# The first query products ahead of the mixing weights, and another engine and bank for the last query chunk

## The chip, the cores and the metric

The kernel runs on one core of a Trainium2 chip. The metric is the device time of one execution in microseconds (us), median of several runs. Engines are named as in the profile: PE is the matrix engine (PEld its weight loads), DVE the vector engine, ACT the scalar engine, POOL the general-purpose engine that issues most loads here, SP the engine that issues the stores.

## The reference

Two blocks follow each other. The first is attention with sorted blocks: batch 4, 8 heads, 768 positions in 8 blocks of 96, head size 64. An 8 x 8 matrix per head is normalised five times by rows and columns, and then mixes the blocks of keys and values:

```
P = sort_net
for _ in range(5):
    P = exp(P - max(P)); P = P / sum over columns; P = P / sum over rows
k_sorted = einsum('bhij,bhjcd->bhicd', P, k_blocks)      # the same for v
scores = q_blocks @ k_sorted^T / sqrt(64)
attn = softmax(scores) @ v_sorted                         # per block of 96
```

The second is a feed-forward block on the 3072 rows of 512 numbers that the attention gives:

```
g = x @ w_gate                       # 512 -> 1536
out = (g * sigmoid(g) * (x @ w_val)) @ w_out              # 1536 -> 512
```

Inputs and output are float32; the kernel casts to bf16 while loading.

## The kernel before, in words

The output is made in eight parts of 384 rows, n = 0 to 7 (a batch and a half each). For each part, `ffn(n)` runs twelve steps m of 128 hidden columns: `gate` (L385, four products into one PSUM bank), `value` (L403), and for the part before it `outp` (L420). Attention units of later parts are merged into this stream by a list of due places (`merge`). All of this is an order written out by hand: PE and POOL run exactly in program order over the whole kernel, DVE and ACT in the prologue.

The prologue makes what part 0 needs from batch 0, in this order on PE:

- `dots(124)` and groups of `fill(idle_ps, n)` (L446): products of zeros whose results nobody reads. The groups stand between single products that read `rowreds[it]` (L455), so that they follow the rounds of normalisation on DVE and ACT.
- `weights(0)`, `weights(1)` (L463): 16 products that spread the normalised matrix `p_bf` into one bank, `w_ps`. `p_bf` is written by DVE in two halves (L214).
- `mix_rows` (L468, DVE): masks `w_ps` into `rmix[0]`, the right-hand side of all value and key products of batch 0. For batches 1 to 3 the same is done later from the same bank, which therefore stays in use until then.
- `q0_chunk(0, 0, 16)` (L254): 32 products with `sel`, a matrix of ones and zeros, that bring query rows into the layout of the scores. They need the load of `q0[0]` (L142) but no mixing weights.
- `v_chunk` six times (L275), `k0_chunk` four times (L264), `q0_chunk(0, 16, 8)` (L254, 16 products), `fill(idle_ps, 4)`, and then the scores `qk` (L307).

Each chunk has a PSUM tile and ends with `drain(eng, ...)`, which copies it to SBUF: `"v"` is DVE (L222), `"s"` is ACT (L224). The last argument names the PSUM tile: `"a"` and `"b"` are pairs of banks with one buffer each, `"gen"` single banks with three buffers in turn. A chunk waits until the drain of the chunk that had its buffer is done. The last chunks of the prologue stand so:

```
k0_chunk(0, 16, "v", "a")
k0_chunk(16, 16, "s", "b")
k0_chunk(32, 8, "v", "gen")
k0_chunk(40, 8, "s", "gen")
q0_chunk(0, 16, 8, "v", "a")
fill(idle_ps, 4)
qk(0, 0, "a")
```

After the scores come exponentials on ACT (L320, L318), attention products `av` (L334), DVE's division (L338, L340), transposes (L351), and the first gate and value products (L519).

POOL issues the loads in program order: the first value rows, `q0[0]` (L142), the first key rows (L149), three copies of value rows (L124), and then the weights of `gate` and `value` in twelve loads of 256 columns (L111), with other loads between. The last two of them hold the columns of steps m = 10 and 11. After the first few, each issue waits until an older load has landed.

Of the kernel before, what the change touches and what calls it, by code (L numbers as in the profile page):

```python
# [17 lines left out]
def kernel(  # L18
# [201 lines left out]
    def drain(eng, dst, src):  # L220
        if eng == "v":
            nc.vector.tensor_copy(dst, src)  # L222
        else:
            nc.scalar.copy(dst, src)  # L224
# [3 lines left out]
    def kqt_tile(b):  # L228
        if b not in kqts:
            kqts[b] = kqp.tile([128, 2 * H2 * NB * C + 32], BF16, name=f"kqt{b}", tag="kqt")  # L230
        return kqts[b]
# [3 lines left out]
    def chunk_tile(name, n, tag):  # L235
        return pair_tile(name, tag) if n == 2 else bank_tile(name, tag)
# [12 lines left out]
    def q0_chunk(t, at, n, eng, tag):  # L249
        dst = kqt_tile(0)[:, GI * C:2 * GI * C].rearrange("p (g t r c) -> p t g r c", g=H2, t=2, c=QC)[:, t]  # L250
        tp = chunk_tile("tq0", n // 8, tag).rearrange("p (l g r) -> p l g r", l=n, g=H2)
        for lc in range(n):
            for two in range(2):
                nc.tensor.matmul(tp[two * D:(two + 1) * D, lc], lhsT=q0[t][:, at + lc, :],  # L254
                                 rhs=sel[:, two], start=True, stop=True)
        drain(eng, dst[:, :, :, at:at + n], tp.rearrange("p l g r -> p g r l"))

    def k0_chunk(at, n, eng, tag):
        dst = kqt_tile(0)[:, 0:GI * C].rearrange("p (n a c) -> p a n c", a=2, c=HC)
        rm = rmix[0].rearrange("p a (g two) i -> p two a g i", two=2)  # L260
        tp = chunk_tile("tk0", n // 8, tag).rearrange("p (l a n) -> p l a n", l=n, a=2)
        for lc in range(n):
            for two in range(2):
                nc.tensor.matmul(tp[two * D:(two + 1) * D, lc].rearrange("p a (g i) -> p a g i", g=H2),  # L264
                                 lhsT=k0[:, at + lc, :], rhs=rm[:, two], start=True, stop=True)
        drain(eng, dst[:, :, :, at:at + n], tp.rearrange("p l a n -> p a n l"))

    def v_chunk(b, at, n, eng, tag):
        rows = slice(0, 128) if b % 2 else lowr
        dst = vt_tile(b // 2)[:, b % 2]  # L270
        mix = rmix[b][rows, 0].rearrange("p a b -> p (a b)")
        tp = chunk_tile("tv", n // 8, tag).rearrange("p (l n) -> p l n", n=H * NB)
        for ld in range(n):
            col = (at + ld) * C
            nc.tensor.matmul(tp[:, ld, :], lhsT=vch[rows, col:col + 128], rhs=mix,  # L275
                             start=True, stop=True)
        drain(eng, dst[:, :, at:at + n], tp[0:C].transpose([0, 2, 1]))
# [166 lines left out]
    def fill(tile, n):  # L444
        for _ in range(n):
            nc.tensor.matmul(tile, lhsT=warm_sb[:, 0:128], rhs=warm_sb, start=True, stop=True)  # L446

    def dots(n):
        for _ in range(n):
            nc.tensor.matmul(idle_ps[0:32, 0:32], lhsT=warm_sb[:, 0:32], rhs=warm_sb[:, 0:32],  # L450
                             start=True, stop=True)

    dots(124)
    for it, n in ((1, 3), (2, 4), (3, 4), (4, 4)):
        nc.tensor.matmul(idle_ps[0:NB, 0:NB], lhsT=rowreds[it][:, :, 0], rhs=rowreds[it][:, :, 0],  # L455
                         start=True, stop=True)
        fill(idle_ps, n)
# [3 lines left out]
    def weights(half):  # L461
        for i in range(NB):
            nc.tensor.matmul(w_ps[halves[half], i].rearrange("p b h -> p (b h)"),  # L463
                             lhsT=p_bf[:, i].rearrange("p a b -> p (a b)"),
                             rhs=ident[0:BH, 0:BH], start=True, stop=True)

    def mix_rows(dst, rows, b):
        nc.vector.tensor_tensor(dst, mask[rows].unsqueeze(2).to_broadcast([R, H, NB]),  # L468
                                w_ps[rows, :, b].transpose([0, 2, 1]), op=ALU.mult)

    weights(0)
    weights(1)
    mix_rows(rmix[0][lowr, 0], lowr, 0)
    mix_rows(rmix[0][highr, 1], highr, 0)
    q0_chunk(0, 0, 16, "s", "b")
    v_chunk(0, 0, 8, "v", "gen")
    v_chunk(0, 8, 8, "s", "gen")
    v_chunk(0, 16, 16, "v", "a")
# [4 lines left out]
    k0_chunk(16, 16, "s", "b")  # L483
    k0_chunk(32, 8, "v", "gen")
    k0_chunk(40, 8, "s", "gen")
    q0_chunk(0, 16, 8, "v", "a")
    fill(idle_ps, 4)
    qk(0, 0, "a")
    qk(0, 1, "b")
# [165 lines left out]
```

## Time and profile before

| | |
|---|---|
| median of 3 runs | 248.58 us (248.43 to 248.70) |
| the profiled execution | 249.62 us |
| its span (first to last instruction) | 247.7 us |
| PE busy | 239.4 us, 97% of the span |
| DVE busy | 157.1 us, 63% |
| ACT busy | 109.5 us, 44% |
| POOL busy | 51.9 us, 21% |
| DMA | 24.38 MB, mean 98 GB/s |

Times in the trace count from the start of the span. A row of the timeline gives start and length, engine, line, operation and tiles, and in brackets how long the engine had been idle before it and which event ended that. Rows that follow each other with the same line and form are put together, with their number behind an x. Products on PE are pipelined: a row's length holds one full latency, and the next row starts before it ends. The profiled execution is one run with the profiler on; its own time stands beside its span because other runs need not agree with it in every part.

### The profile page before, as it was taken

Reading aid. Unit: us, or ns where it says so; the run is one execution under the profiler, and the core shown is the slowest. Engines: PE = TensorE matmul, PEld = TensorE weight load, DVE = VectorE, ACT = ScalarE, POOL = GpSimd, SP = SyncE. Lnnn points to the kernel's source line nnn. Section 1 sums busy time; section 2 is a strip of 40 time slices with the busy share of each in tenths; the row PEclk is TensorE's granted clock in tenths of the full one; section 3 lists DMA queues with packets and bytes.
Section 4 is the critical chain, followed back from the end, with each engine's and each line's share of the span. In section 5 each row is a group of like instructions: output and inputs, shape, how many; then the busy total and the mean of one; then the engine's idle time right before and its main releaser. Section 6 shows DMA issues by size and latency. Waiting matters only on the chain.

```text
span 247.7 us, 6185 instructions
## 1 busy us (share of the span) xinstructions
PE 239.4 (97%) x2633; PEld 140.7 (57%) x2633; DVE 157.1 (63%) x332; ACT 109.5 (44%) x186; POOL 51.9 (21%) x45
## 2 busy tenths in 40 slices
PE   8799998999999999999999999999999999999995
PEld 6375665666555556655555655565555555555543
DVE  6686789787556775857657646755764585446700
ACT  3877652453544444444642552354245334232311
POOL 5993459960049300000000000000000000000000
PEclk9999999999999999999999999999999999999999
DMA  5999999999999287010122121112111121100122
GB/s 98 214 120 181 218 191 219 194 227 215 215 164 179 41 201 173 4 42 3 45 56 52 55 62 34 44 42 78 32 42 45 39 57 54 42 21 25 42 81 88
DMA packets 39578, 24.38 MB, mean 98 GB/s; under 512 B 27712, under 2 KB 35648, under 8 KB 39104
## 3 DMA queue, kind: packets, MB, share of 16 engines
q0 software_dynamic: 21376, 14.16, 39.3%
q1 hardware_dynamic: 18176, 9.84, 13.9%
q8 instruction: 20, 0.33, 0.5%
q14 instruction: 6, 0.05, 0.1%
HBM read 28.32 MB, written 7.86 MB: 146 GB/s over the span
## 4 chain that ended last, share of the span: by engine, by line
PE 83%; DVE 9%; ACT 2%; issue 2%; DMA 2%; DVEq 0%; POOLq 0%
PE v_ps L403 23%; PE o_ps L420 23%; PE g_ps L385 22%; PE tkq L244 3%; PE av_ps L334 2%; PE qk L307 2%; DVE st L340 2%; DMA v<-in_v_dram 2%; DVE gs_sb L395 2%; DVE h L408 2%; DVE vt L222 1%; PE o_ps L436 1%; PE idle_ps L446 1%; PE tv L275 1%; ACT th_sb L393 1%
## 5 line engine op out<-in xcount | busy, mean ns | idle before, releaser
L395 DVE SCALAR_TENSOR_TENSOR gs_sb<-th_sb,g_ps 128x384 bf16<-128x384 bf16 x96 | 52.8, 550 | 51.5 <-ACT th_sb L393 48.7
L403 PE MATMUL v_ps<-xt,wv_sb 128*128 128x384 bf16 x380 | 77.3, 326 | 1.1 <-DVE st L340 0.7
L385 PE MATMUL g_ps<-xt,wg_sb 128*128 128x384 bf16 x376 | 76.7, 326 | 0.1
L393 ACT ACTIVATE th_sb<-g_ps 128x384 bf16<-128x384 f32 x96 | 47.1, 490 | 57.0 <-PE g_ps L385 54.5
L420 PE MATMUL o_ps<-wo_sb,h 128*128 128x512 bf16 x276 | 64.0, 379 | 0.0
L408 DVE SCALAR_TENSOR_TENSOR h<-v_ps,gs_sb 128x384 bf16<-128x384 f32 x96 | 53.3, 555 | 6.9
L403 PEld LDWEIGHTS <-wv_sb 128*128 128x128 bf16 x380 | 35.1, 97 | 24.9 <-issue 1.9
L385 PEld LDWEIGHTS <-wg_sb 128*128 128x128 bf16 x376 | 34.7, 97 | 23.5 <-issue 0.4
L420 PEld LDWEIGHTS <-h 128*128 128x128 bf16 x276 | 26.3, 98 | 28.9
L425 ACT COPY o_sb<-o_ps 128x512 f32<-128x512 f32 x23 | 13.5, 585 | 50.9 <-PE o_ps L420 50.9
L124 POOL COPY vch<-v 64x1536 bf16<-64x1536 bf16 (+2 forms) x11 | 28.6, 2635 | 21.1 <-DMA v<-in_v_dram 21.0
L320 ACT ACTIVATE e_all<-qk 96x768 bf16<-96x768 f32 x30 | 22.6, 802 | 7.6 <-PE qk L307 7.6
L340 DVE TENSOR_TENSOR st<-av_ps,r_sb 96x512 bf16<-96x512 f32 x32 | 21.7, 679 | 0.2
L334 PEld LDWEIGHTS <-e_all 96*128 96x128 bf16 x256 | 12.0, 97 | 4.9 <-ACT e_all L320 0.9
L334 PE MATMUL av_ps<-vt,e_all 96*128 96x65 bf16 x256 | 13.2, 193 | 0.0
L222 DVE CAST vt<-tv 96x1024 bf16<-96x1024 f32 (+1 forms) x9 | 9.8, 1096 | 2.6 <-PE tv L285 1.6
L338 DVE RECIPROCAL r_sb<-av_ps 96x8 f32<-96x8 f32 x32 | 6.4, 199 | 8.0 <-PE av_ps L334 7.9
L224 ACT CAST vt<-tv 96x1024 bf16<-96x1024 f32 (+1 forms) x9 | 8.1, 913 | 3.0 <-PE tv L285 1.8
L446 PE MATMUL idle_ps<-warm_sb 128*128 128x512 bf16 x25 | 7.7, 416 | 0.0
L222 DVE COPY oh_sb<-o_ps 128x256 f32<-128x256 f32 x1 | 0.4, 423 | 9.3 <-PE o_ps L436 9.3
L122 ACT COPY vch<-v 64x768 bf16<-64x768 bf16 (+1 forms) x4 | 5.4, 1375 | 0.7 <-DMA v<-in_v_dram 0.7
L370 POOL DMA_DIRECT2D q_scr<-in_q_dram x2 | 5.7, 3228 | 0.0
(80 smaller groups left out, 135.3 us busy)
## 6 DMA issues: line engine op xcount, KB each, us to landing
out_dram<-o_sb SPq DMA_DIRECT2D x23, 256.0 KB, 2.0
v<-in_v_dram POOLq DMA_DIRECT2D x3, 768.0 KB, 19.9
wg_sb<-in_moe_w_gate_dram POOLq DMA_DIRECT2D x6, 256.0 KB, 11.1
wv_sb<-in_moe_w_val_dram POOLq DMA_DIRECT2D x6, 256.0 KB, 11.9
wo_sb<-in_moe_w_out_dram POOLq DMA_DIRECT2D x1, 1536.0 KB, 23.8
kp<-in_k_dram POOLq DMA_DIRECT2D x2, 768.0 KB, 15.1
q_scr<-in_q_dram POOLq DMA_DIRECT2D x2, 768.0 KB, 29.9
v<-in_v_dram POOLq DMA_DIRECT2D x2, 384.0 KB, 6.4
```

The lines of the kernel that those rows point to most:

```text
L124: eng.tensor_copy(dst, src.transpose([0, 2, 1]))
L222: nc.vector.tensor_copy(dst, src)
L320: nc.scalar.activation(e_all[:, n:n + 2, 0:4 * C], wide[0:C, :, 0:4 * C], AF.Exp, scale=scale)
L334: nc.tensor.matmul(o[:, two, i4, 0:D + 1], lhsT=e[:, i4 * C:i4 * C + 128], rhs=vt[:, 2 * g + two, half * 4 + i4, 0:D + 1], start=True, sto ...
L340: nc.vector.tensor_tensor(st.rearrange("p i two d -> p two i d"), o[0:C, :, :, 0:D], r_sb.to_broadcast([C, 2, 4, D]), op=ALU.mult)
L385: nc.tensor.matmul(g_ps, lhsT=wg_sb[:, kc, ts(m, 128)], rhs=xt[:, kc, :], start=(kc == 0), stop=(kc == NKC - 1))
L393: nc.scalar.activation(th_sb, g_ps, AF.Tanh, scale=0.5)
L395: nc.vector.scalar_tensor_tensor(gs_sb, th_sb, 1.0, g_ps, op0=ALU.add, op1=ALU.mult)
L403: nc.tensor.matmul(v_ps, lhsT=wv_sb[:, kc, ts(m, 128)], rhs=xt[:, kc, :], start=(kc == 0), stop=(kc == NKC - 1))
L408: nc.vector.scalar_tensor_tensor(h_tiles[n][:, m, :], v_ps, 0.5, gs_tiles.pop(m), op0=ALU.mult, op1=ALU.mult)
L420: nc.tensor.matmul(o_ps, lhsT=h_w[:, m, ts(t3, 128)], rhs=wo_sb[:, m, :], start=(m == 0), stop=(m == NFC - 1))
L425: nc.scalar.copy(o_sb, o_ps)
```

## The change

The group of unread products after the last round of normalisation shrinks from four to one. `q0_chunk(0, 0, 16, "s", "b")` moves from behind the mixing rows to ahead of `weights(0)`, with its engine and its banks as before. The last query chunk of the prologue, `q0_chunk(0, 16, 8)`, is drained by ACT in place of DVE and takes a bank of `"gen"` in place of the pair `"a"`.

```diff
     dots(124)
-    for it, n in ((1, 3), (2, 4), (3, 4), (4, 4)):
+    for it, n in ((1, 3), (2, 4), (3, 4), (4, 1)):
         nc.tensor.matmul(idle_ps[0:NB, 0:NB], lhsT=rowreds[it][:, :, 0], rhs=rowreds[it][:, :, 0],
                          start=True, stop=True)
         fill(idle_ps, n)
...
+    q0_chunk(0, 0, 16, "s", "b")
     weights(0)
     weights(1)
     mix_rows(rmix[0][lowr, 0], lowr, 0)
     mix_rows(rmix[0][highr, 1], highr, 0)
-    q0_chunk(0, 0, 16, "s", "b")
     v_chunk(0, 0, 8, "v", "gen")
...
     k0_chunk(40, 8, "s", "gen")
-    q0_chunk(0, 16, 8, "v", "a")
+    q0_chunk(0, 16, 8, "s", "gen")
     fill(idle_ps, 4)
     qk(0, 0, "a")
```

On PE the 32 query products stand before the 16 weight products, and all else keeps its order. DVE loses one drain and ACT gains one, at the same place in its order. POOL and SP issue the same transfers in the same order.

## Prediction

> **What bounds the kernel now.** I read the page first (engines, then the chain that ended last), then the timeline of the first 20 us, where the change lies, then the landings of the loads, and last the places where TensorE (PE) still stands idle after that.
>
> ```profile
> PE 239.4 (97%) x2633; PEld 140.7 (57%) x2633; DVE 157.1 (63%) x332; ACT 109.5 (44%) x186; POOL 51.9 (21%) x45
> ...
> PE 83%; DVE 9%; ACT 2%; issue 2%; DMA 2%; DVEq 0%; POOLq 0%
> ```
>
> PE is busy nearly all the time and makes most of the chain. So a step of the prologue counts only if it moves the moment at which PE's dense stream runs on. The timeline (start, length, engine, line, operation, tiles) around the change:
>
> ```profile
> 10.46 1.04 PE L446 MATMUL idle_ps<-warm_sb 128*128 128x512 bf16 x4
> 11.04 0.74 DVE L214 TENSOR_TENSOR p_bf<-p_ps,colred 32x256 bf16<-32x256 f32 x2
> ...
> 11.51 0.77 PE L463 MATMUL w_ps<-ident,p_bf 32*64 32x32 bf16 x16
> ...
> 12.20 0.70 PE L254 MATMUL tq<-sel,qk 128*64 128x64 bf16 x32
> 12.31 0.47 DVE L468 TENSOR_TENSOR rmix<-mask,w_ps 64x64 bf16<-64x64 bf16 x2 [0.53 <-PE w_ps L463]
> ...
> 12.83 2.27 PE L275 MATMUL tv<-rmix,vch 64*128 64x64 bf16 x64
> ...
> 13.27 2.52 DVE L222 CAST vt<-tv 96x512 bf16<-96x512 f32 x3 [0.49 <-PE tv L275]
> ...
> 15.25 1.92 PE L264 MATMUL tk<-rmix,qk 128*64 128x64 bf16 x96
> ...
> 15.98 1.82 DVE L222 CAST kqt<-tk 128x1024 bf16<-128x1024 f32 x2 [0.19 <-PE tk L264]
> 16.70 1.50 ACT L224 CAST kqt<-tk 128x1024 bf16<-128x1024 f32 x2 [0.30 <-PE tk L264]
> ...
> 17.26 0.44 PE L254 MATMUL tq<-sel,qk 128*64 128x64 bf16 x16
> ...
> 17.63 1.04 PE L446 MATMUL idle_ps<-warm_sb 128*128 128x512 bf16 x4
> 17.73 0.69 DVE L222 CAST kqt<-tq 128x512 bf16<-128x512 f32 x1
> ```
>
> The reader sees a relay: weights, mixing rows, value products, and then VectorE (DVE) draining one product bank after another almost without a pause from 13.27 to 18.42. The scores (L307) start at 18.60, behind four unread products. Later there is one large idle stretch of PE. The weight-load row of the timeline there says:
>
> ```profile
> 41.99 0.44 PEld L403 LDWEIGHTS <-wv_sb 128*128 128x128 bf16 x4 [0.84 <-DMA wv_sb<-in_moe_w_val_dram]
> ```
>
> PE's own row at 42.00 shows 0.70 us idle and names DVE; the landing is the better reading: this load, issued at 26.90, takes 15.1 us by the DMA view, so it lands at 42.0. PE had ended its transposes at 41.31. The kernel's first 42 us are thus tied to a stream of loads as well as to the prologue.
>
> **The change part by part.**
>
> *Three unread products go.* They are the last of the four at 10.46, about 0.22 us each (1.04 is three spacings and one full 0.38). They end where the weights begin at 11.51, and those wait for p_bf, not for them. Removed: nothing on the path.
>
> *The first query group moves ahead of the weights.* It now waits for its load: issued at 3.00, 7.8 us to landing, 10.8. A release takes some 0.05 us (DVE's drain of 1024 ends at 15.98 + 1.22 = 17.20, the waiting products start at 17.26), so it starts at 10.85. From its first start to that of the next group were 12.83 - 12.20 = 0.63 us, so PE is free at 11.48, before p_bf releases the weights at 11.51. Queued behind this wait are the weights, on which DVE waits. The margin is larger than 0.03: the second half of p_bf releases the fifth weight product only at 11.84, and four of them need little over 0.1, so the landing may come 0.24 later (about 11.04) at no cost. [...] The row has 0.63 us with the change of group, 20 ns each, and I take the row.
>
> *The value products come earlier.* They stood behind the query group until 12.83. Now they wait only for the first mixing row: 12.31 plus half of 0.47, plus the release, 12.58. That is 0.25 earlier. Other conditions hold: GpSimd's copy of the value rows (9.47 + 2.81 = 12.28), ScalarE's (ACT's) copies (12.18), the key rows (second load 4.05 + 10.4 = 14.5, needed at 15.0). ACT drains the first query group from 12.2 instead of 12.94, off the path. So DVE's relay shifts as a whole: the key drains start at 15.73 and end at 15.98 + 1.82 - 0.25 = 17.55.
>
> *The last query chunk changes its bank, and here the change pays.* It used the pair "a", free when DVE had drained the first key chunk (17.20). Now it takes a bank of "gen". There are three; the mixing weights hold one until DVE's last mixing row, and the other two pass in turn from value chunks to key chunks. The one it gets was that of the third key chunk, which DVE drains last, until 17.55. So the chunk starts at 17.60, against 17.26: 0.34 later, although PE has had nothing else to do since 16.9. The 0.25 gained and 0.34 more are gone: the step from one drain to the next (17.80 - 17.20 = 0.60) replaces the earlier start.
>
> *ACT drains it instead of DVE.* The same size from the key chunk takes ACT 0.59 (17.61, in a narrower window). Products end at 17.60 + 0.44 = 18.04, so the drain runs from 18.08 to 18.67. The four unread products now run from 17.97, and the scores behind them start at 18.60 + 0.34 = 18.94. They cover the drain with 0.22 to spare; were they not there, the scores would start at 18.72. DVE saves 0.69, but what follows on it (mixing rows of other batches) has no waiter there.
>
> *Sum of the prologue.* Scores 0.34 us late. From here on exponentials, attention products, DVE and transposes follow in the same order; no engine's order changes, no load moves: GpSimd's queue has the same order and its waits are for landings, not for PE. So the delay arrives at 41.31 as at most 0.34, at 41.65. The weights land at 42.0. PE's wait shrinks from 0.70 to 0.36, and the stream goes on at 42.00 as before. DVE is still 0.2 late there (copy ends at 43.06, product h by 43.6), and that ends at 44.03, where it had 0.61 us idle. Net zero: 249.62 for the profiled execution (span 247.7 and 1.9 around it), as before. The runs have a median of 248.58, 1.04 lower, and I keep that distance: 248.6.
>
> The unknown is the cover in runs without a profile. If the load stream lands up to 0.36 earlier there, nothing changes; if 0.70 earlier, the whole 0.34 shows, 248.9. Below nothing: if the bank wait were absent, the prologue would gain at most 0.25, which without cover gives 248.3.
>
> **The rivals.**
>
> *Cover gone (248.9).* The 1.04 us between profile and median may be partly this wait. Against: loads keep the DMA queues full from 10 to 80 us and the last of twelve weight loads would have to land 0.7 earlier in 29 us of stream. Still inside 0.2%.
>
> *The bank is free earlier (248.3 to 248.6).* It needs the chunk to get another "gen" bank. The order in which the banks are taken speaks against it; the cover would hide it too.
>
> *Slower: the first query rows land late.* One place, the weight load of the first query product, with all 16 mixing weights behind it. Each us beyond 11.04 is a us for weights, mixing rows and all drains. The landings come in a row (9.4, 10.8, 12.7, 14.5), 1.4 to 1.9 apart, so a shift of 0.4 is no rarity. With full cover it decides from a landing at 11.9 (0.34 + 0.86 - 0.70 = 0.50), without cover from 11.2; at 11.3 without cover 0.34 + 0.26 = 0.60, so 249.2.
>
> *Slower: the clock falls.* Three dense products fewer. The first unread products (4.86, 1.46 for three) ran at about half speed, so one stage such as the key products would cost some 1.9 more: about 250. Against: the small value and key products from 12.8 to 17.2 kept full speed, and 0.96 us of idle at 8.66 did not lower it.
>
> **How the numbers follow.** 0.2% is 0.50 us, about what a measurement of this kernel can tell from no change. Forecast, delay under cover, 248.6: 0.45. Cover gone: 0.19, of which 0.04 above 0.2%. Bank free: 0.08, of which 0.02 below -0.2%. Late query rows: 0.14. Clock: 0.06. Loads landing earlier for a reason I don't see: 0.08. Slower 0.04 + 0.14 + 0.06 = 0.24; faster 0.02 + 0.08 = 0.10; same 0.66. Range: 248.2 (bank free without cover, and 0.1 for the spread of the runs) to 249.2 (late rows); the clock, half of the late rows and part of the earlier loads are left out.
>
> **What would show it.** Right: first query products at 10.85, value products at 12.58, last query chunk at 17.60 with some 0.6 us of idle PE before it, scores at 18.94, the wait at 42.0 about 0.36, DVE's idle at 44.03 down to 0.4, all later rows in place. Wrong: weights after 11.51, the last chunk before 17.5, a last value load that lands before 41.7, or unread products longer than 0.38.

## The result, and the profile after

The changed kernel is slower: 249.99 us median of 14 executions (248.86 to 252.17) against 248.55 of 14 (248.43 to 249.91); ratio 1.0058, 95% interval [1.0035, 1.0081]. The forecast of no change was wrong, and so was the range. What stands out first is not the median but the spread: 3.3 us for one and the same program. Beside each time stands the mean granted clock of PE (the share of full speed that the chip lets PE run at, from the profile), and the two go together:

| mean granted clock | executions | time, us |
|---|---|---|
| 0.998 to 1.000 | 2 | 248.86, 249.09 |
| 0.991 to 0.993 | 6 | 249.37 to 250.27, median 249.57 |
| 0.985 to 0.986 | 3 | 250.57 to 251.19, median 251.12 |
| 0.979 | 3 | 251.55 to 252.17, median 251.73 |

One stretch of 3.41 us at half speed lowers the mean over 247 us by 0.5 x 3.41 / 247 = 0.7%; the levels fit none, one, two and three such stretches. One is in the profile below, at a mean of 0.992; two are in that of e3, at 0.986; three are worked out from the mean alone.

The profiled execution (249.39 us, span 247.4) has one: the clock reads 0.68 from 14.90 to 15.00, 0.50 from there to 18.30 and 0.76 from 18.30 to 18.40, which is 0.06 + 3.30 + 0.05 us at half speed. The page of the changed kernel, its engines and its slices:

```profile
PE 237.0 (96%) x2606; PEld 141.5 (57%) x2630; DVE 156.4 (63%) x331; ACT 110.3 (45%) x187; POOL 51.9 (21%) x45
...
PE   6689999999999999999999999999999999999994
...
PEclk9979999999999999999999999999999999999999
```

The one 7 in the row of the clock is the third slice (12.4 to 18.6 us); the row of before has only nines. The windows view of the changed kernel (busy time of PE, PEld, DVE, ACT, POOL, then the clock) places it:

```profile
11.50:14.90 3.40, 2.88 (x99) 2.76 (x97) 2.68 (x5) 2.48 (x4) 3.40 (x6) 1.00 0.68 112
14.90:18.30 3.40, 3.00 (x107) 2.85 (x101) 2.84 (x6) 2.38 (x5) 3.40 (x6) 0.51 1.24 159
18.30:21.70 3.40, 3.20 (x48) 1.55 (x48) 0.74 (x2) 2.67 (x5) 1.15 (x2) 0.99 1.16 178
```

Before, over the first two of these stretches:

```profile
11.50:14.90 3.40, 3.28 (x112) 3.02 (x112) 2.33 (x5) 2.17 (x3) 3.40 (x5) 1.00 0.51 88
14.90:18.30 3.40, 3.14 (x123) 2.50 (x119) 3.21 (x5) 2.99 (x4) 3.40 (x6) 1.00 1.38 181
```

Most of the prologue's key products and the last query chunk run at half clock in the changed kernel. The timeline of the changed kernel, the rows that answer to those of before:

```profile
10.11 0.39 PE L446 MATMUL idle_ps<-warm_sb 128*128 128x512 bf16 x1
...
10.69 0.74 DVE L214 TENSOR_TENSOR p_bf<-p_ps,colred 32x256 bf16<-32x256 f32 x2
...
10.69 0.70 PE L254 MATMUL tq<-sel,qk 128*64 128x64 bf16 x32 [0.19 <-DMA qk<-in_q_dram]
...
11.31 0.60 PE L463 MATMUL w_ps<-ident,p_bf 32*64 32x32 bf16 x16
...
11.95 0.47 DVE L468 TENSOR_TENSOR rmix<-mask,w_ps 64x64 bf16<-64x64 bf16 x2 [0.53 <-PE w_ps L463]
...
12.22 2.26 PE L275 MATMUL tv<-rmix,vch 64*128 64x64 bf16 x64 [0.30 <-DVE rmix L468]
...
14.62 2.64 PE L264 MATMUL tk<-rmix,qk 128*64 128x64 bf16 x96
15.53 2.03 DVE L222 CAST kqt<-tk 128x1024 bf16<-128x1024 f32 x2 [0.37 <-PE tk L264]
...
17.61 0.64 PE L254 MATMUL tq<-sel,qk 128*64 128x64 bf16 x16 [0.35 <-DVE kqt L222]
...
18.29 0.59 ACT L224 CAST kqt<-tq 128x512 bf16<-128x512 f32 x1 [0.35 <-PE tq L254]
...
19.21 0.69 PE L307 MATMUL qk<-kqt 64*128 64x96 bf16 x24
```

Normalisation ended 0.35 earlier here (p_bf at 10.69 against 11.04), because the first value rows landed earlier (ACT starts to copy them at 6.14 here, and at 6.54 before, after 0.67 us of waiting for the load); so rows are compared by their distance from p_bf. Value products: 12.22 - 10.69 = 1.53 against 1.79, the 0.26 that was forecast. The 96 key products take 2.64 against 1.92. The scores stand 8.52 behind p_bf, against 7.56: 0.96 later, where 0.34 was forecast.

And the wait at 42 us, which was to hide the delay, is not in this execution. PE's timeline there:

```profile
41.58 0.34 PE L351 MATMUL x_ps<-ident,st 96*128 96x96 bf16 x4
41.75 0.81 PE L403 MATMUL v_ps<-xt,wv_sb 128*128 128x384 bf16 x4
```

The last value load was issued at 26.16 and took 13.7 us by the DMA view: it lands at 39.9, some 2 us earlier than in the profile of before (0.7 of this because it was issued earlier), and PE does not wait for it.

### The profile page after: what moved, and what is told of

It reads as the page before. It is cut to its first block, busy times and chain, and to the rows that moved or that the text cites. A ratio compares the mean times of both kernels' runs of the same rounds, so it can differ in the third digit from the quotient of the medians.

```text
span 247.4 us, 6154 instructions
## 1 busy us (share of the span) xinstructions
PE 237.0 (96%) x2606; PEld 141.5 (57%) x2630; DVE 156.4 (63%) x331; ACT 110.3 (45%) x187; POOL 51.9 (21%) x45
## 4 chain that ended last, share of the span: by engine, by line
PE 83%; DVE 7%; DMA 3%; issue 3%; ACT 2%; POOL 1%; DVEq 0%; POOLq 0%
PE v_ps L403 23%; PE g_ps L385 23%; PE o_ps L420 22%; DMA qk<-in_q_dram 3%; PE tkq L244 3%; PE av_ps L334 3%; PE qk L307 2%; DVE st L340 2%; DVE gs_sb L395 2%; DVE h L408 1%; DVE vt L222 1%; PE o_ps L436 1%; PE tv L275 1%; PE tk L264 1%; PE tq L254 1%
## 5 line engine op out<-in xcount | busy, mean ns | idle before, releaser
L420 PE MATMUL o_ps<-wo_sb,h 128*128 128x512 bf16 x255 | 61.4, 379 | 1.3 <-issue 0.3
L446 PE MATMUL idle_ps<-warm_sb 128*128 128x512 bf16 x19 | 5.5, 381 | 0.4 <-issue 0.4
```

The source lines that it names most:

```text
L420: nc.tensor.matmul(o_ps, lhsT=h_w[:, m, ts(t3, 128)], rhs=wo_sb[:, m, :], start=(m == 0), stop=(m == NFC - 1))
```

## The experiments

Theory after the result: two costs add up. The clock falls for stretches of the prologue because the unread dense products are gone, and the last chunk waits for its bank. Rivals: the new order itself, late query rows, or ACT's drain. The kernels fall into three groups, e1 to e4, e5 to e8 and e9 to e11, each with executions of before beside it (medians 248.55, 248.83 and 248.63); the ratio is to these and need not be the quotient of the medians. "Below" counts executions with a mean clock under 0.994; over the three groups before had 1 of 86.

| kernel | median, us | ratio [95%] | below | lowest |
|---|---|---|---|---|
| e1 order alone | 249.77 | 1.0033 [1.0002, 1.0064] | 9 of 12 | 248.14 |
| e2 bank and ACT alone | 249.09 | 1.0028 [1.0017, 1.0040] | 0 of 11 | 249.00 |
| e3 fewer unread alone | 250.64 | 1.0087 [1.0069, 1.0106] | 6 of 6 | 250.35 |
| e4 changed, pair a | 250.61 | 1.0075 [1.0045, 1.0104] | 6 of 6 | 249.18 |
| e5 changed, four unread kept | 249.28 | 1.0007 [0.9979, 1.0036] | 4 of 12 | 249.05 |
| e6 changed, unread in gaps | 249.14 | 1.0029 [1.0007, 1.0051] | 2 of 12 | 248.82 |
| e7 the same, pair a | 249.02 | 0.9998 [0.9968, 1.0027] | 2 of 12 | 248.30 |
| e8 before, small unread | 249.12 | 1.0012 [0.9980, 1.0045] | 2 of 12 | 248.41 |
| e9 order, free unread | 248.65 | 0.9997 [0.9977, 1.0016] | 1 of 12 | 248.26 |
| e10 changed, early unread | 249.92 | 1.0046 [1.0023, 1.0069] | 8 of 12 | 248.84 |
| e11 order, more unread | 248.52 | 1.0000 [0.9978, 1.0022] | 0 of 12 | 248.35 |

The medians of the second group are not to be read finely: it ran on another chip, and before itself spread from 248.39 to over 251 there at full clock. The lowest times and the counts are steadier.

### The parts one by one: e1, e2, e3

```diff
e1  (on the changed kernel)
-    q0_chunk(0, 16, 8, "s", "gen")
+    q0_chunk(0, 16, 8, "v", "a")
e2  (on before)
-    q0_chunk(0, 16, 8, "v", "a")
+    q0_chunk(0, 16, 8, "s", "gen")
e3  (on before)
-    for it, n in ((1, 3), (2, 4), (3, 4), (4, 4)):
+    for it, n in ((1, 3), (2, 4), (3, 4), (4, 1)):
```

> First half of the change alone: the query group ahead of the weights, one unread product in place of four there; the last query chunk as before (DVE, pair a). Theory 'clock and bank': the clock falls here as in the changed kernel, because the three dense products are gone (mean granted clock under 0.995 in most executions, each window at half speed some 0.9 us), but the bank wait is not there: scores 0.25 earlier than before at full clock, so executions at clock 1.000 near 248.3 and the median between 248.6 and 249.8. Theory 'bank alone': 248.3 and the clock at 1.000 throughout. Theory 'late query rows': first query product later than p_bf's first half, weights delayed, slower by that amount at any clock.

> Second half alone: order and unread products as before, the last query chunk drained by ACT from a gen bank. Theory 'clock and bank': the chunk starts when DVE has drained its last key chunk, 17.80 in place of 17.20, so the scores are 0.60 later than before; clock mostly 1.000; median 248.6 to 249.2 depending on what the last value load hides. Theory 'fewer dense products are all': as before, 248.55. If the clock falls here too, then the idle stretch ahead of the last chunk is enough for it, and the median is above 249.3.

> Only the unread products: one in place of four behind the last round of normalisation, all else as before. PE's useful work starts at the same times. Theory 'clock by dense products': the clock falls in most executions, median 249.0 to 250.5, with PE's small products of the prologue at twice their spacing in the profile. Theory 'the order matters, not the unread products': 248.55 and clock 1.000.

e3 shows what the unread products do. Nothing in it moves but three products that nobody reads, and it costs 2.1 us: the dearest of all parts, with the clock low in all six executions. Its windows view, cut at the changes of the clock:

```profile
10.10:13.50 3.40, 2.52 (x75) 2.02 (x76) 2.21 (x9) 2.62 (x3) 3.40 (x3) 1.00 0.78 157
13.50:16.90 3.40, 3.40 (x88) 3.31 (x86) 2.26 (x4) 2.34 (x4) 3.40 (x6) 0.50 0.97 121
16.90:20.30 3.40, 3.07 (x81) 2.36 (x78) 3.13 (x6) 1.54 (x3) 2.38 (x4) 0.50 1.08 148
20.30:23.70 3.40, 3.37 (x61) 1.82 (x60) 1.50 (x5) 2.38 (x5) 1.30 (x2) 1.00 1.39 192
```

PE was busy for 2.52 of 3.40 us, and then two stretches follow at half speed, though PE is busy throughout the first of them. Of the 0.88 us of idle, 0.2 is the end of a wait that before has too; the rest is a new hole, in e3's timeline:

```profile
11.47 0.77 PE L463 MATMUL w_ps<-ident,p_bf 32*64 32x32 bf16 x16 [0.65 <-DVE p_bf L214]
...
15.77 2.77 PE L264 MATMUL tk<-rmix,qk 128*64 128x64 bf16 x96
```

0.65 us of waiting where the unread products had stood. The key products, wholly at half clock here, take 2.77 us in place of 1.92. In before a stretch at the same place had PE busy for 3.29 of 3.41:

```profile
10.26:13.67 3.41, 3.29 (x83) 2.36 (x84) 2.22 (x9) 2.65 (x3) 3.41 (x4) 1.00 0.76 155
```

e1 has the gain and the loss side by side. At full clock three executions lie at 248.14 to 248.20, some 0.37 under before's median of 248.55 and 0.27 under its lowest time of 248.41: the query group ahead of the weights does help, by the 0.25 forecast or a little more. But the clock falls in 9 of 12. The rival of late query rows is out as far as three executions show it: nothing slow is left at full clock.

e2 is the bank. No clock falls, and the time is 249.09, 0.54 over before. Its timeline:

```profile
17.57 0.44 PE L254 MATMUL tq<-sel,qk 128*64 128x64 bf16 x16 [0.68 <-DVE kqt L222]
```

PE stands for 0.68 us until DVE has drained its last key chunk. 0.60 was the step from one drain to the next; nearly all of it reaches the end.

e2 also holds a second lesson. Its hole is as long as e3's 0.65, and PE's busy time around it is as low:

```profile
14.26:17.67 3.41, 2.56 (x123) 2.35 (x120) 3.19 (x5) 2.75 (x4) 3.41 (x6) 1.00 1.32 169
```

A stretch of 3.41 us that begins with the hole, at 16.89, holds the 0.68 us and the 0.16 before the unread products at 18.17, so PE is busy for 2.57 us of it at most. Yet the clock fell in 0 of 11 executions, against 6 of 6 in e3. So neither the length of the hole nor PE's busy time decides alone; where the hole lies, or which products surround it, matters too, and which of the two is not shown. In e2 these products are mostly key products, in e3 mixing weights, query and value products.

### ACT's drain without the bank: e4

```diff
-    q0_chunk(0, 16, 8, "s", "gen")
+    q0_chunk(0, 16, 8, "s", "a")
```

> The changed kernel with the last query chunk on pair a, still drained by ACT. Theory 'clock and bank': the chunk starts 0.6 earlier than in the changed kernel; ACT's drain then waits for ACT's own last key drain, so the scores gain some 0.4; executions at full clock near 248.4, median 249.2 to 249.8 because the clock still falls. Theory 'ACT's drain is the cost': no gain over the changed kernel, 249.99.

The median is not lower but 0.6 higher than that of the changed kernel: all six executions had one to three low stretches (mean clock 0.993 to 0.979). At the same clock they lie under the changed kernel's medians (249.25 against 249.57 at one stretch, 250.61 against 251.12 at two, 251.56 against 251.73 at three), by 0.2 to 0.5, so the pair seems to help; with only six executions and none at full clock this one is weak evidence.

### Unread products put back: e5, e6, e7

```diff
e5  (on the changed kernel)
-    for it, n in (..., (4, 1)):
+    for it, n in (..., (4, 4)):
e6  (on the changed kernel)
-    for it, n in (..., (4, 1)):
+    for it, n in (..., (4, 2)):
...
     weights(1)
+    fill(idle_ps, 1)
...
+    fill(idle_ps, 2)
     q0_chunk(0, 16, 8, "s", "gen")
e7  (as e6, but)
+    fill(idle_ps, 1)
+    q0_chunk(0, 16, 8, "s", "a")
```

> The changed kernel with the four unread products kept where before has them. Theory 'clock by dense products': the clock stays at 1.000 in most executions, although the order is the changed one and PE's small products are the same. At full clock the query group starts some 0.6 later than in the changed kernel, the value products about 0.2 later than before, and the bank wait adds 0.6: 249.2 to 249.5, a narrow spread. Theory 'the order lowers the clock': clocks of 0.979 to 0.993 and a spread of 3 us as in the changed kernel.

> The changed kernel with the removed unread products put back where PE is idle: two behind the last round of normalisation, one between the weights and the value products, two more ahead of the last query chunk. Theory 'clock by dense products': clock at 1.000 in most executions and 248.8 to 248.9, the changed kernel's time at full clock. If windows of 3.4 us still fall short, a part of the executions stays at 0.979 to 0.993 and the median is 249 to 250.

> As the kernel with unread products in the gaps, but the last query chunk on pair a, drained by ACT, and one unread product ahead of it. Theory 'clock and bank': at full clock 0.5 to 0.6 below the changed kernel's 248.86, so 248.2 to 248.4, faster than before by 0.1%. Theory 'ACT's drain costs': not below 248.5.

e5 keeps the changed order and has the clock low in 4 of 12, and never for more than one stretch (mean clock 0.992), where the changed kernel had 12 of 14 and up to three. So it is mainly the unread products, not the order, though the rest of the change is not quite innocent: before had 1 of 86. e6 shows the changed kernel's own work without the clock: lowest 248.82, close to its 248.86 at full clock, 0.3 to 0.4 over before. Its rows say the same:

```profile
10.94 0.74 DVE L214 TENSOR_TENSOR p_bf<-p_ps,colred 32x256 bf16<-32x256 f32 x2
...
17.49 0.44 PE L254 MATMUL tq<-sel,qk 128*64 128x64 bf16 x16
...
18.83 0.69 PE L307 MATMUL qk<-kqt 64*128 64x96 bf16 x24
```

The scores stand 7.89 behind p_bf, against 7.56 before: 0.33 later. That is the 0.34 of the forecast's sum, and no cover takes it away. In e7 six of the ten executions at full clock lie at 248.30 to 248.53: level with before, not the 0.2 below that was expected. The other four, at 250.02 to 250.60, are part of a second scatter at full clock, of which e8 shows one source. ACT's drain as the cost is not borne out: four executions of e7 lie below 248.5, and its lowest, 248.30, is close to the 248.26 of e9 below, where DVE drains.

### Busy or dense: e8

```diff
-    for it, n in (..., (4, 4)):
+    for it, n in (..., (4, 1)):
...
+    dots(24)
```

> Before, with three of the four unread dense products (128 x 128 by 512 columns) replaced by 24 unread small ones (32 x 32 by 32 columns) that keep PE busy for about the same 0.65 us. Theory 'the clock goes by busy time': 248.55 at clock 1.000, as before. Theory 'it goes by how much of the array works': the clock falls as in the kernel with fewer unread products, median 250 to 251.

Small products hold the clock nearly as well: 10 of 12 at full clock, lowest 248.41, against none of six without them; PE was busy for 3.28 of the 3.40 us from 11.20 in its profile. So in this stretch it is mostly a matter of PE standing idle, not of the dense form. Not wholly: 2 of 12 fell. The profiled execution (249.99 us, clock 1.000) shows something else, one source of the scatter at full clock:

```profile
42.35 0.82 PE L403 MATMUL v_ps<-xt,wv_sb 128*128 128x384 bf16 x4 [0.98 <-DMA wv_sb<-in_moe_w_val_dram]
```

Here the wait at 42 us is back, 0.98 us long. Of the thirteen profiled executions three have it: before (249.62 us in all), e8 (249.99) and e11 (250.06, with 1.00 us). In these the last value load landed at 42.0 to 42.3 us, in the other ten at 38.7 to 40.0. All three are long for executions at full clock; in e8 the wait is a good half of the 1.6 us above its lowest time. That the long executions without a profile have the same wait is likely but not shown.

### Which stretch, and a version without the losses: e10, e9, e11

```diff
e10 (on the changed kernel)
-    for it, n in ((1, 3), (2, 4), (3, 4), (4, 1)):
+    for it, n in ((1, 3), (2, 7), (3, 6), (4, 1)):
e9  (on e1)
-    for it, n in ((1, 3), (2, 4), (3, 4), (4, 1)):
+    for it, n in ((1, 3), (2, 7), (3, 6), (4, 2)):
...
     weights(1)
+    fill(idle_ps, 1)
e11 (as e9, but)
+    for it, n in ((1, 3), (2, 7), (3, 6), (4, 3)):
...
+    dots(5)
     k0_chunk(0, 16, "v", "a")
```

> The changed kernel with 7 and 6 unread dense products behind the third and fourth round, and its single one behind the last. Tells which stretch counts. Theory 'each window of 3.4 us by itself': the windows between 10.3 and 18 are as empty as in the changed kernel, so the clock still falls in most executions where a window lies in 11 to 15, perhaps for fewer windows; median 249.4 to 250. Theory 'the total of unread products counts': clock at 1.000, 248.86.

> First half of the change alone (query group ahead of the weights, last chunk as before on DVE and pair a), with unread dense products only where PE stands idle: 7 and 6 in place of 4 and 4 behind the third and fourth round of normalisation, 2 behind the last, 1 between the weights and the value products. Theory 'clock and bank': clock at 1.000 in most executions, full-clock executions near 248.2 (0.3 below before at full clock), median 248.2 to 248.5. If activity counts only after 10.3 us, some executions keep one window at half speed and the median is above 248.8.

> As the first of this call, with 3 unread products behind the last round (query group about 0.1 later) and five small unread products where PE waits for DVE ahead of the key products. Theory 'clock and bank': fewer executions below clock 1.000 than the first; full-clock executions 248.2 to 248.35.

("The first" in the last expectation is e9.) More unread products before 10.3 us do not replace those behind it: e10 falls in 8 of 12, for one or two stretches (mean clock 0.993 and 0.986), no longer three. e9 and e11 keep the clock (1 and 0 of 12), but their full-clock times start at 248.26 and 248.35, no longer at e1's 248.14: the products in the gaps cost 0.1 to 0.2. Neither is faster than before within its interval; e11's 248.52 is level with it. The gain of the order is about what it takes to hold the clock.

## Why the prediction was wrong, point by point

- *Unread products: "nothing on the path".* This is the step that failed: the sum priced their removal at nothing. True by the chain of waits, and beside the point: their effect is on the clock, at half speed for 3.4 us in the changed kernel's profile and for 6.8 us in e3's. e3 measured it alone: +2.1 us.
- *The rival "the clock falls", given 0.06.* It named the right mechanism. The two reasons against it were bad: that the small products kept full speed, which they did in a kernel where a dense group lay just before them; and that 0.96 us of idle at 8.66 did no harm, in a stretch that had eight dense products. No row of before showed the prologue without the group. An operation with no reader in a hand-made order had to be priced by what it may hold up. The slow rows at 4.86 (1.46 us for three dense products, against 1.04 for four at 8.79) were a hint, though the granted clock of before reads 1.00 there too, so that only their length speaks for half speed. That "about 250" meets the median of 249.99 is luck: it took 1.9 more for the key products alone, which at half clock cost 0.85 more (2.77 against 1.92 in e3), and the executions hold none to three whole stretches.
- *Query group 0.63 long, weights not delayed.* Held in effect: the group takes 11.31 - 10.69 = 0.62. The weights start 0.62 behind p_bf, against 0.47 before, so they were 0.15 late; but the margin of 0.24 that the prediction gave them covers it, and the mixing row comes 1.26 behind p_bf against 1.27. The 0.62 us are 19 ns for each of the 32 products; the prediction had 20, from the row of before.
- *Value products 0.25 earlier.* Held: 0.26.
- *The bank: 0.60 later, 0.34 net.* Held: e2 +0.54 for the bank; e6's scores 0.33 later; and the changed kernel's two executions at full clock lie 0.31 and 0.54 over before's median.
- *ACT's drain costs nothing under the four unread products.* Held at full clock: e6 has the scores 1.34 behind the start of the last chunk (17.49 and 18.83), as forecast (17.60 and 18.94).
- *The wait at 42 us hides it.* The second step that failed. It was a property of the one profiled execution, whose loads landed 2 us later than in the next profile; only three of thirteen profiles have it, all of them long executions. The distance of 1.04 us from the median had hinted at it, and the rival "cover gone" was worth more than 0.19.
- *Late query rows, 0.14.* Did not happen: the query group waited 0.19 us for its load, until 10.69, and cost the mixing row nothing.

So of the 1.44 us some 0.3 to 0.5 are bank less order, which the sum had (0.34) but held to be covered, and some 0.9 to 1.1 are clock, which it had not. The division is rough: only two of the changed kernel's executions were at full clock.

What stays open: what in a stretch makes the clock fall. Before a fall PE was busy for 2.52 of 3.40 us in e3, 2.88 in the changed kernel and 3.03 of 3.41 in e10; it was 3.14 or more in the rows of before from 10.3 us on, where the clock stayed up. But e2 kept its clock with 2.56 of 3.41, and before with 2.07 of 3.50 between 6.8 and 10.3 us:

```profile
6.80:10.30 3.50, 2.07 (x10) 0.60 (x8) 2.10 (x11) 3.43 (x5) 3.40 (x2) 1.00 1.06 212
```

There eight dense products ran, in the stretch of e2 shown above none. So neither busy time nor the number of dense products alone fits all of these. The way back is as unclear: e3's stretch at half clock with PE busy for 3.40 of 3.40 us was followed by another at half clock, the changed kernel's with 3.00 by full clock.

## What to carry to other kernels

Before taking out work that nobody reads, ask what it holds up that no wait shows: here the clock of the engine, at half speed for 3.4 us in the changed kernel's profile and for 6.8 in e3's. A wait of the profiled execution counts as cover only if the execution is a typical one; compare its time with the median first, and look at what landed late. When one program's times spread by more than 1%, sort them by clock before comparing medians.

## What the runs showed of the hardware

A hole of 0.65 us more on PE within 3.4 us was enough in e3 for two stretches at half clock or more, in 6 of 6 executions (mean clock 0.980 to 0.986); a hole of 0.68 us some 6 us later, in e2, was not, in 0 of 11. The windows views show the clock at half speed for 3.41 us in the changed kernel and for 6.80 in e3, and at 1.00 on either side. Why one program has none of these stretches in some executions and up to three in others is not shown. Gaps of 0.2 to 0.7 us within one stretch of 3.4 us were enough in e3 (2.52 of 3.40 us busy).

The landing of one load, the last of the value weights, lay between 38.7 and 42.3 us in the thirteen profiled executions; it was issued between 25.1 and 27.2.
